# Attention plus spectral mixing on one core: folded maxima scans and eight spectral blocks moved into the attention loop

## The chip, the cores and the metric

The kernel runs on one core of one Trainium2 chip. The metric is the device time of one execution in microseconds (us); a kernel's time is the median of its runs. The core has five instruction queues that run side by side and wait for each other through semaphores: PE (TensorE, matmuls), DVE (VectorE), ACT (ScalarE), POOL (GpSimd) and SP (SyncE, which here only issues DMAs). Each queue is in order: an instruction that waits holds back everything behind it on its queue. A DMA can be issued from any of SP, ACT and POOL and stands in that queue like any other instruction.

## The reference

```python
S, D, H = 2048, 512, 32; Dh = 16
g = sigmoid((x * gate_w).sum(-1, keepdims=True))
# A: attention with 32 heads of 16
q, k, v = split_heads(x @ wqkv)
p = softmax(q @ k.T * Dh ** -0.5)
a = (p @ v merged over heads) @ wo
# B: spectral mixing, real part of a two-dimensional Fourier transform
ar = x @ dft_hid_re.T ; bi = x @ dft_hid_im.T
b = dft_seq_re @ ar - dft_seq_im @ bi
return g * a + (1 - g) * b
```

`x` is 2048 x 512. `dft_seq_re` and `dft_seq_im` are 2048 x 2048, so B is two products of 2048 x 2048 with 2048 x 512 behind two small ones. All arrays are float32.

## The kernel before

**Arithmetic.** A float32 operand that is multiplied with accuracy is split in two fp32r parts, hi (a rounding copy) and lo (raw minus hi), and a product is made of three: hi hi, hi lo, lo hi. A product over 128 rows is issued as two matmuls over rows 0 to 63 and 64 to 127 (`halves_of`, L145), which run in the array side by side into two PSUM halves. Such a pair of 512 columns is the unit in which PE time is counted below, and is called a pair. In the first part of the program each pair belongs to a "slot": `products` issues one pair and calls `beside`, which counts the slot, runs deferred actions that have come due (`after(n, f)`: do f n slots later) and sprinkles in other work.

**The maxima.** The softmax needs a shift for each query and head, the row maximum of its scores. It is computed by a pass of its own, called a scan. Heads go in 16 pairs; a pair's pass is 64 scans (`SCANS`), each of a block of 128 queries against 512 keys (`i // 4` is the query block, `i % 4` the key chunk). A scan (`scan`, L119 and L121) is two matmuls of 48 rows, one for each head of the pair (one pair in the sense above), and one DVE tensor_reduce over the 2 x 512 scores from PSUM into `mx`. After a pair's 64 scans `shift` (L134 to L138) reduces `mx` to the maxima, splits and stores them. There are 16 x 64 = 1024 scans (`TOTAL`). The rows of queries and keys that scans read are loaded from DRAM for each head pair into two 1 MB tiles of the pool `stk` by eight DMAs (`row_loads`, L87).

**Front, first half.** Projections: queries and keys transposed (`project_t`, 32 calls of 12 slots, results added, split and stored to `q_d`, `k_d`), values, and the two hidden-dimension transforms (`project_s`, 48 calls of 12 slots). Each call's two PSUM halves are evacuated by ACT and added by POOL.

**Front, second half.** The spectral product: 16 blocks of output rows in phase 0 (`dft_seq_re`) and 16 in phase 1 (`dft_seq_im`), 48 slots each. The coefficients come in units of 4 row blocks (12 slots): a 256 KB load on SP, then a cast and a subtraction on POOL (`prepare`, L246 and L247). The transformed operand lies in 32 SBUF blocks, `ah[s]` and `al[s]`; between the phases they are rewritten block by block (`split_operand`, L213 and L214, on ACT, DVE and POOL). At a block's end ACT scales both halves by 1 - g (L496, L500), POOL adds them and, in phase 1, adds the phase 0 result read back from `y_d` (L450, L452); SP stores the sum to `y_d` (`mixed`).

**Scans beside the front.** From slot 192 on, `beside` issues a scan every `PACE` = 3.9 slots (other spacings hold in a few stretches), with two PSUM tiles of two banks each, until `FRONT` = 564 scans are done.

**Attention loop.** 512 steps: 16 head pairs x 32 (`PERIODS`), each a half of the queries against a block of 128 keys for two heads. A step computes scores transposed in four matmuls (`qk2`, L543), three exponentials on ACT (one of 1024 columns, L547, two of 512, L551) and `pv` (L558). The remaining scans run here, one to a step (`next_scan`), so steps 0 to 459 have one. From step `MIX` = 461 on there is no scan; every step takes one piece of the output mixing instead (`fill`, the generator `outputs`: `mix_heads`, `mix_some`), and `pv` is issued for two steps together on every second step. The scan and the mixing share one PSUM tile of two banks (`pair_banks`). A short tail closes the program.

Of the kernel before, what the change touches and what calls it, by code (L numbers as in the profile page):

```python
# [10 lines left out]
F32 = mybir.dt.float32  # L11
F32R = mybir.dt.float32r
# [6 lines left out]
P = 128  # L19
S = 2048  # L20
# [14 lines left out]
FRONT = 564  # L35
PACE = 3.9
NWARM = 20
MIX = TOTAL - FRONT + 1
SLOW = 3


def build(tc, x, xT, wqkv, wo, wrT, wiT, cr, ci, gate, out):
    nc = tc.nc
    with ExitStack() as ctx:
        keep = ctx.enter_context(tc.tile_pool(name="keep", bufs=1))
        stk = ctx.enter_context(tc.tile_pool(name="stk", bufs=6))
        sm = ctx.enter_context(tc.tile_pool(name="sm", bufs=2))
        dram = ctx.enter_context(tc.tile_pool(name="dram", bufs=1, space=DRAM))

        q_d = [dram.tile([P, 2, S], F32, name=f"q_d{f}") for f in range(ND)]  # L50
        k_d = [dram.tile([P, 2, S], F32, name=f"k_d{f}") for f in range(ND)]
        m_d = [dram.tile([2, 4, 2, NB, 32], F32, name=f"m_d{p}") for p in range(NP)]
# [23 lines left out]
        def row_loads(p, queue):  # L76
# [4 lines left out]
            for j in range(2):  # L81
                b, r = 64 * j, slice(DH * ((2 * p + j) % 8), DH * ((2 * p + j) % 8) + DH)
                loads += [(ks[b:b + 32, :], k_d[p // 4][r, 0:1, :].to_broadcast([DH, 2, S])),
                          (qs[b:b + 32, :], q_d[p // 4][r, :, :].rearrange("e n s -> (e n) s")),
                          (ks[b + 32:b + 48, :], k_d[p // 4][r, 1, :]),
# [23 lines left out]

        def scan(n, ps):  # L110
# [4 lines left out]
            if i == 0:  # L115
                mx[p] = sm.tile([P, 2, NB, 4], F32, tag="mx", name="mx")
# [4 lines left out]
            nc.vector.tensor_reduce(mx[p][:, :, qb, c], ps, axis=AX.X, op=ALU.max)  # L121

        def shift(p):
# [6 lines left out]
            def store():  # L130
                for n, s in enumerate((hi, lo)):
                    nc.sync.dma_start(m_d[p][n].rearrange("g j b k -> (g j b) k"), s.bitcast(F32))

            return [lambda: nc.vector.tensor_reduce(m, mx[p].rearrange("p j b c -> p (j b) c"), axis=AX.X, op=ALU.max,  # L134
                                                    negate=True),
# [10 lines left out]


        seen, slots, due = [0], [0], []
        pace = [None, 0.0]
        with ExitStack() as pf:  # L150
            psf = pf.enter_context(tc.tile_pool(name="psf", bufs=2, space=PSUM))
            big = pf.enter_context(tc.tile_pool(name="big", bufs=1, reuse_waits="tile"))
            cw = pf.enter_context(tc.tile_pool(name="cw", bufs=4, reuse_waits="tile"))

            def s1():
                return psf.tile([P, 2, 512], F32, tag="s1", name="s1")
# [5 lines left out]
            def after(n, f, *args):  # L162

                due.append((slots[0] + n, len(due), f, args))
# [10 lines left out]
            def load_scan_beside(p):  # L175
                scanned[p], loads = row_loads(p, nc.scalar if p else nc.sync)
# [6 lines left out]
            def beside():  # L183
# [5 lines left out]
                pace[1] += 1.0 / pace[0]  # L189
                while seen[0] < FRONT and pace[1] >= 1.0:  # L190
                    pace[1] -= 1.0
                    n = seen[0]
                    if n % SCANS == 36:
                        load_scan_beside(n // SCANS + 1)
                    scan(n, s1())
                    seen[0] += 1
                    if seen[0] % SCANS == 0:
                        for d, part in enumerate(shift(n // SCANS)):
                            after(3 + 4 * d, part)
# [654 lines left out]
```

## Time and profile before

| | us |
|---|---|
| median of 3 runs | 1753.88 (1752.49 to 1754.19) |
| the profiled execution, its own time | 1756.16 |
| its span (first to last instruction) | 1754.4 |
| PE busy / DVE busy / ACT busy / POOL busy | 1731.9 / 1347.4 / 1166.8 / 777.5 |

Busy time of PE is not PE at its peak: matmuls are pipelined and their ends are modelled, so a stage is read by how many matmuls it got through. The three stages that matter are the first half of the front (up to 284.8 us), the second half (to 736.1 us) and the attention loop with its tail. L numbers are line numbers of the kernel before.

### The profile page before, as it was taken

Reading aid. Unit: us, or ns where it says so; the run is one execution under the profiler, and the core shown is the slowest. Engines: PE = TensorE matmul, PEld = TensorE weight load, DVE = VectorE, ACT = ScalarE, POOL = GpSimd, SP = SyncE. Lnnn points to the kernel's source line nnn. Section 1 sums busy time; section 2 is a strip of 40 time slices with the busy share of each in tenths; the row PEclk is TensorE's granted clock in tenths of the full one; section 3 lists DMA queues with packets and bytes.
Section 4 is the critical chain, followed back from the end, with each engine's and each line's share of the span. In section 5 each row is a group of like instructions: output and inputs, shape, how many; then the busy total and the mean of one; then the engine's idle time right before and its main releaser. Section 6 shows DMA issues by size and latency. Waiting matters only on the chain.

```text
span 1754.4 us, 33571 instructions
## 1 busy us (share of the span) xinstructions
PE 1731.9 (99%) x13640; PEld 988.3 (56%) x13640; DVE 1347.4 (77%) x1296; ACT 1166.8 (67%) x1894; POOL 777.5 (44%) x881
## 2 busy tenths in 40 slices
PE   8999999999999999999999999999999999999998
PEld 6987787878777787633333333333333333333554
DVE  6799999999999999866666666666666777765233
ACT  6445333000031000299999999999999999999885
POOL 3688557666677777413232322323232323323222
PEclk9999999999999999999999999999999999999999
DMA  7662455525474553633233351441433333453512
GB/s 263 224 199 74 128 156 177 138 92 133 129 188 134 136 150 112 145 61 62 58 63 61 57 99 25 87 72 42 79 66 61 65 67 72 85 108 91 138 41 100
DMA packets 119307, 185.79 MB, mean 106 GB/s; under 512 B 53184, under 2 KB 55728, under 8 KB 112240
## 3 DMA queue, kind: packets, MB, share of 16 engines
q1 hardware_dynamic: 77200, 148.96, 32.7%
q0 software_dynamic: 38496, 19.47, 5.3%
q10 hardware_dynamic: 3456, 15.21, 4.1%
q8 instruction: 107, 1.75, 0.5%
q14 instruction: 48, 0.39, 0.1%
HBM read 129.89 MB, written 53.22 MB: 104 GB/s over the span
## 4 chain that ended last, share of the span: by engine, by line
PE 80%; DVE 12%; DMA 3%; POOL 2%; issue 1%; ACT 1%; SPq 0%; DVEq 0%; ACTq 0%; POOLq 0%
PE pvb L558 27%; PE xy L145 21%; PE s L543 18%; PE s L119 11%; DVE mx L121 11%; PE s L145 3%; DMA lc<-ob 2%; POOL s L173 1%; POOL el L173 0%; DVE b L214 0%; DMA q_d<-eh 0%; DMA raws<-xT 0%; DMA raws<-wqkv 0%; POOL lc L566 0%; DVE y L645 0%
## 5 line engine op out<-in xcount | busy, mean ns | idle before, releaser
L121 DVE TENSOR_REDUCE mx<-s 128x2 f32<-128x1024 f32 x1024 | 1208.4, 1220 | 276.2 <-PE s L119 276.1
L551 ACT ACTIVATE e<-s 128x512 f32<-128x512 f32 x1024 | 630.4, 748 | 1.6 <-PE s L543 1.6
L547 ACT ACTIVATE eb<-s 128x1024 f32<-128x1024 f32 x512 | 600.2, 1172 | 23.0 <-PE s L543 23.0
L558 PE MATMUL pvb<-e,va 128*17 128x512 f32 x2048 | 528.5, 599 | 0.0
L558 PE MATMUL pvb<-eb,va 128*17 128x512 f32 x2048 | 528.3, 599 | 0.0
L543 PE MATMUL s<-qs,ks 50*128 50x512 f32 x2048 | 454.1, 442 | 0.0
L543 PEld LDWEIGHTS s<-qs,ks 50*128 50x128 f32 x2048 | 215.3, 184 | 418.4 <-ACT eb L547 389.5
L119 PE MATMUL s<-ks,qs 48*128 48x512 f32 x2048 | 418.7, 397 | 8.4 <-DVE mx L121 6.9
L496 ACT ACTIVATE tx<-xy,gm 128x512 f32<-128x512 f32 x32 | 22.1, 689 | 380.6 <-PE xy L145 329.7
L119 PEld LDWEIGHTS s<-ks,qs 48*128 48x128 f32 x2048 | 200.3, 184 | 45.5 <-DVE mx L121 20.0
L566 POOL DMA_DIRECT2D lc<-ob x124 | 63.1, 515 | 238.9 <-DVE ob L563 238.8
L558 PEld LDWEIGHTS pvb<-eb,va 128*17 128x17 f32 x2048 | 63.4, 95 | 174.9 <-issue 163.7
L573 POOL DMA_DIRECT2D r_d<-lc x31 | 18.1, 585 | 322.3 <-DVE lc L572 322.3
L145 PE MATMUL xy<-w,b 64*128 64x512 f32 x768 | 105.4, 392 | 0.2 <-ACT s L292 0.2
L645 DVE SCALAR_TENSOR_TENSOR y<-s,g,y 128x512 f32<-128x512 f32 x50 | 36.6, 748 | 81.5 <-PE s L145 80.9
L310 ACT ACTIVATE tx<-xy 128x512 f32<-128x512 f32 x48 | 28.7, 598 | 93.1 <-PE xy L145 91.5
L575 POOL DMA_DIRECT2D rb<-r_d x124 | 60.3, 493 | 54.0 <-DMA r_d<-lc 53.9
L145 PEld LDWEIGHTS xy<-w,b 64*128 64x128 f32 x768 | 72.9, 186 | 17.0 <-ACT s L292 0.7
L576 POOL TENSOR_TENSOR ob<-ob,rb 128x512 f32<-128x512 f32 x31 | 39.7, 1282 | 70.6 <-DMA rb<-r_d 68.8
L408 POOL TENSOR_TENSOR ab<-tx,ty 128x512 f32<-128x512 f32 x32 | 41.3, 1291 | 50.6 <-ACT ty L311 32.2
L558 PEld LDWEIGHTS pvb<-e,va 128*17 128x17 f32 x2048 | 63.3, 95 | 0.3 <-ACT e L551 0.3
L173 POOL TENSOR_TENSOR el<-s,eh 128x512 fp32r<-128x512 f32 x32 | 41.4, 1295 | 48.2 <-ACT eh L173 41.0
(928 smaller groups left out, 2085.8 us busy)
## 6 DMA issues: line engine op xcount, KB each, us to landing
craw<-ci SPq DMA_DIRECT2D x64, 256.0 KB
craw<-cr SPq DMA_DIRECT2D x60, 256.0 KB
ks<-k_d SPq DMA_DIRECT2D x48, 256.0 KB
qs<-q_d SPq DMA_DIRECT2D x48, 256.0 KB
ab_d<-ab SPq DMA_DIRECT2D x32, 256.0 KB
y_d<-y SPq DMA_DIRECT2D x32, 256.0 KB
o_d<-oh POOLq DMA_DIRECT2D x28, 256.0 KB, 9.8
o_d<-ol POOLq DMA_DIRECT2D x28, 256.0 KB, 15.3
```

The costliest lines, as they stand in the source:

```text
L119: nc.tensor.matmul(ps[:, j, :], qs[b:b + 48, qb * P:(qb + 1) * P], ks[b:b + 48, c * 512:(c + 1) * 512], start=True, stop=True)
L121: nc.vector.tensor_reduce(mx[p][:, :, qb, c], ps, axis=AX.X, op=ALU.max)
L145: nc.tensor.matmul(ps[j], lhs[r], rhs[r], start=first, stop=last)
L173: d[2](*d[3])
L408: nc.gpsimd.tensor_add(ab, tx, ty)
L543: nc.tensor.matmul(pss[j], ks[b:b + 50, kb * P:(kb + 1) * P], qs[b:b + 50, q0:q0 + 512], start=True, stop=True)
L547: nc.scalar.activation(e, ps, AF.Exp, scale=SCALE)
L551: nc.scalar.activation(e[j], pss[j], AF.Exp, scale=SCALE)
L558: nc.tensor.matmul(pvb[r:r + VC, :], va[:, kb, 2 * p + j, :], es[c][j], start=kb == 0, stop=kb == NB - 1, tile_position=(0, r))
L566: nc.gpsimd.dma_start(lc[32 * n:32 * n + 32, :], ob[r + DH:r + VC, :].rearrange("p (s e) -> p s e", e=16))
L575: nc.gpsimd.dma_start(rb[r:r + DH, :], r_d[p][h][n:n + 1, :].to_broadcast([DH, 512]))
L576: nc.gpsimd.tensor_mul(ob, ob, rb)
```

## The change

**Folded scans.** For head pairs 3 to 10, as far as they are scanned in the front, the maximum over two key chunks is taken by max(s1, s2) = max over columns of (relu(s1 - s2) + s2). The keys of chunk c - 1 (c odd) are replaced by the difference of chunk c - 1 and chunk c, so the matmul of an even chunk gives s1 - s2. ACT takes its relu into SBUF, and the matmul of the odd chunk is finished by one DVE tensor_tensor_reduce of 512 columns (add, then maximum, with an accumulator output) in place of a reduction. The difference keys are made in the front (`fold_keys`) and stored to a second DRAM array `kf_d`. The two heads of a pair are offset by one scan, so each folded scan issues one even and one odd matmul, one relu and one tensor_tensor_reduce, in four single PSUM banks.

**Pace.** `FRONT` becomes 692. Plain scans still go at 3.9 slots (5.2 during the key projections, 4.5 in other narrow stretches), folded ones at 2.18.

**Moved blocks.** The last eight blocks of phase 1 leave the front and become filling of the attention loop: steps 333 (`MIX`) to 460 each take three slots of them, the output mixing starts at step 461 (`OUT`) as before. Their coefficients are split on DVE, their result is taken in by two DVE scalar_tensor_tensor per block.

**Others.** Head pair 10, which is folded for 52 scans, is loaded again with plain keys at the head of the attention loop. The output weights and rows go to the operand's SBUF blocks as those come free. One key projection moves behind the query projections, and the value weights' split moves from POOL to DVE.

```diff
+LATER = 8
+FRONT = 564 + 16 * LATER
 PACE = 3.9
+FOLDED = range(3 * SCANS, FRONT)
+FOLD_PACE = 2.18
+SLOW_PACE = 5.2
+NARROW = 4.5
 MIX = TOTAL - FRONT + 1
+OUT = MIX + NB * LATER
...
+        def scan_folded(n, j, bank, pool):
+            p, i = n // SCANS, n % SCANS
+            qb, c = i // 4, i % 4
...
+            b, ps = 64 * j, bank(f"{'dk'[c % 2]}{j}")
+            nc.tensor.matmul(ps, qs[b:b + 48, qb * P:(qb + 1) * P], ks[b:b + 48, c * 512:(c + 1) * 512],
+                             start=True, stop=True)
+            if c % 2 == 0:
+                fold[j] = pool.tile([P, 512], F32, tag=f"fold{j}", name="fold")
+                nc.scalar.activation(fold[j], ps, AF.Relu)
+            else:
+                nc.vector.tensor_tensor_reduce(out=fold[j], in0=ps, in1=fold[j], scale=1.0, scalar=-3.0e38,
+                                               op0=ALU.add, op1=ALU.max, accum_out=mx[p][:, j, qb, c // 2:c // 2 + 1])
...
-                pace[1] += 1.0 / pace[0]
+                pace[1] += (PACE / FOLD_PACE if seen[0] in FOLDED else 1.0) / pace[0]
...
+                    if n not in FOLDED:
+                        done = scan_plain(n)
+                    else:
+                        scan_folded(n, 0, *beds)
+                        done = behind(n - 1)
...
+            coef = coef[:len(coef) - NU * LATER]
...
+                def fold_keys(f, c):
+                    a, b = half.pop(c - 1), half.pop(c)
+                    hi = ep.tile([P, 512], F32R, tag="eh", name="eh", bufs=3)
+                    lo = ep.tile([P, 512], F32R, tag="ty", name="fl")
+                    nc.gpsimd.tensor_sub(a, a, b)
...
+                    after(7, nc.scalar.copy, hi, a)
+                    after(12, (nc.vector if f else nc.gpsimd).tensor_sub, lo, a, hi.bitcast(F32))
+                    after(13, store, 0, hi)
+                    after(16, store, 1, lo)
...
                     def store(i, v):
                         nc.sync.dma_start(dst[f][:, i, c * 512:(c + 1) * 512], v.bitcast(F32))
+                        if folded and c % 2:
+                            nc.sync.dma_start(kf_d[f][:, i, c * 512:(c + 1) * 512], v.bitcast(F32))
...
+                psk = py.enter_context(tc.tile_pool(name="psk", bufs=1, space=PSUM, reuse_waits="tile"))
+                beds += [lambda tag: psk.tile([P, 512], F32, tag=tag, name="s"), cp]
...
-                            nc.scalar.mul(ty, pss[t][1], gm[:, t:t + 1])
-                        after(5, mixed, ph, t, yre.get(t), tx, ty)
+                            after(5, nc.scalar.mul, ty, pss[t][1], gm[:, t:t + 1])
+                        after(10, mixed, ph, t, yre.get(t), tx, ty)
...
+            def split_unit():
+                if raws:
+                    raw = raws.pop(0)
...
+                    nc.vector.tensor_copy(hi, raw)
+                    nc.vector.tensor_sub(lo, raw, hi.bitcast(F32))
+                    parts.append((hi, lo))
+
+            def spectral(t):
+                ps = pair_banks()
+                y = ap.tile([P, D], F32, tag="take", name="y", bufs=3)
+                nc.sync.dma_start(y, y_d[t // 4][:, t % 4, :])
+                for s in range(NB):
+                    if s % CS == 0:
+                        hi, lo = parts.pop(0)
+                        load_unit()
+                    if s % CS == 1:
+                        split_unit()
+                    w = s % CS
+                    for i, (c_, a_) in enumerate(((hi, ah[s]), (hi, al[s]), (lo, ah[s]))):
+                        halves_of((ps[:, 0, :], ps[:, 1, :]), c_[:, w, :], a_, s == 0 and i == 0, s == NB - 1 and i == 2)
+                    if s < NB - 1:
+                        yield
+                for j in range(2):
+                    nc.vector.scalar_tensor_tensor(y, ps[:, j, :], gm[:, t:t + 1], y, op0=ALU.mult, op1=ALU.add)
+                nc.sync.dma_start(y_d[t // 4][:, t % 4, :], y)
+                yield
...
             def outputs():
+                for t in range(NB - LATER, NB):
+                    yield from spectral(t)
                 for c in range(NC):
...
+            if FRONT % SCANS:
+                load_scan(FRONT // SCANS)
...
-                if step >= MIX - 150 and step % 8 == 0:
+                if step >= OUT - 12:
                     next(operands, None)
-                if step == MIX - 12:
+                if step in (OUT - 12, OUT - 4):
+                    output_rows((step - OUT + 12) // 8)
```

More of the change, by code (lines that the diff above doesn't have):

```diff
@@ L74, in build, with row_loads @@
         scanned, used = {}, {}
-        def row_loads(p, queue):
+        def row_loads(p, queue, keys=k_d):
             qs = stk.tile([P, S], F32R, tag="stk", name="qs")
@@ L605, in output_operands @@
                     yield
[L606 removed]
+                    w = [block(12 + 2 * n + i) for i in range(2)]
                     nc.vector.tensor_copy(w[0], raw)
@@ L629, in output_rest @@
             def output_rest(h):
-                a = [ap.tile([P, 512], F32R, name=f"or{h}{i}") for i in range(2)]
+                a = [block(24 + 2 * h + i) for i in range(2)]
                 for i in range(2):
```

148 lines of the change are left out of this document (100 added, 48 removed).

## Prediction

> **What bounds the kernel now.** I read the page's busy times first, then the two rows of its slices that change, then the busy times of the stages.
>
> ```profile
> PE 1731.9 (99%) x13640; PEld 988.3 (56%) x13640; DVE 1347.4 (77%) x1296; ACT 1166.8 (67%) x1894; POOL 777.5 (44%) x881
> ...
> DVE  6799999999999999866666666666666777765233
> ACT  6445333000031000299999999999999999999885
> ```
>
> ```profile
> 0.00:284.80 284.80, 277.83 (x2332) 230.69 (x2334) 257.40 (x261) 134.83 (x268) 174.79 (x142) 1.00 0.56 178
> 284.80:736.10 451.30, 447.43 (x3814) 358.29 (x3812) 445.69 (x408) 52.52 (x85) 308.94 (x304) 1.00 0.50 136
> 736.10:1617.50 881.40, 877.74 (x6464) 331.84 (x6464) 599.01 (x564) 877.65 (x1388) 265.72 (x395) 1.00 0.36 69
> 616.00:660.00 44.00, 44.00 (x382) 35.62 (x380) 44.00 (x40) 3.81 (x6) 31.53 (x32) 1.00 0.56 145
> 1000.00:1200.00 200.00, 200.00 (x1482) 75.75 (x1476) 135.80 (x127) 200.00 (x318) 64.29 (x96) 1.00 0.34 66
> ```
>
> The columns are the stretch, its length, and the busy time of PE, PE's weight loads, DVE, ACT and POOL with their instruction counts, then clock and DMA. A PE at 99% everywhere says little, so I go by counts. The second half of the front is 451.3 us with PE and DVE both full and ACT at 52.5. Its best stretch gets 382 matmuls through in 44 us: a pair costs 44 / 191 = 0.2304 us. The stage holds 1536 slots and 370 scans, 1906 pairs, so 439.3 us of PE; 12.0 us are lost. The attention loop has ACT at 200 of 200 us: 318 exponentials at three to a step are 106 steps, 1.887 us each (over the whole stage 1388 / 3 = 462.7 steps, 1.905 each). There the scans cost no time: DVE and PE both have room.
>
> **The front's second half, PE.** The order of the two programs' instructions shows 1152 slots there in place of 1536, and 507 scans (7 plain, 500 folded) in place of 370: 1659 pairs, 382.2 us, 57.1 less than 439.3. That is the gain if no other engine sets the rate. In the folded stretch a scan comes every 3.18 to 3.2 pairs, 0.733 us. Each scan now needs one relu on ACT and one tensor_tensor_reduce (TTR) on DVE, and the program has that as two DVE instructions: the main one of 512 columns and an accumulator read of 128x1. Neither is in this trace. The nearest rows (from the views by line, by group, the chain of waits and the timeline):
>
> ```profile
> 291.48 69.34 DVE mx L121 x61
> L173 DVE TENSOR_TENSOR s<-xy,tx x11: 678/691/694, 16.3 to 54.2; 128x512 f32<-128x512 f32 x11
> L645 DVE SCALAR_TENSOR_TENSOR y<-s,g,y x50: 735/751/752, 1621.2 to 1748.6; 128x512 f32<-128x512 f32 x50
> 1745.93 3.37 DVE L645 SCALAR_TENSOR_TENSOR y<-s,g,y 128x512 f32<-128x512 f32 x5
> 284.70 0.20 DVE L136 STREAM_TRANSPOSE mt<-m 128x32 f32<-128x32 f32 x1
> 284.82 1.19 DVE L121 TENSOR_REDUCE mx<-s 128x2 f32<-128x1024 f32 x1
> L381 ACT ACTIVATION_READ_ACCUMULATOR xg<-xg x16: 186/203/208, 126.0 to 179.3; 128x1 f32 x16
> L214 DVE TENSOR_TENSOR b<-early,b x6: 681/1383/1782, 493.0 to 503.3; 128x512 fp32r<-128x512 f32 x6
> ```
>
> Rows with three numbers give minimum, median and maximum in ns. A plain scan's reduction takes 69.34 / 61 = 1.137 us of DVE. Five scalar_tensor_tensor in a row take 3.37 us at 0.751 each, so the next starts after (3.37 - 0.75) / 4 = 0.655: 0.096 of each is hidden. A two-source op with one source in PSUM is 0.691 or 0.751, so the main part costs 0.595 to 0.655; I take the middle, 0.625. A short op lets the next start 0.12 later (284.70 to 284.82); I take that for the accumulator read, since it has the shortest row of all. A TTR is then 0.745 us. Ends: 0.595 (the read wholly hidden) and 0.751 + 0.203 = 0.954 (nothing hidden, the read as long as ACT's). The subtraction with both sources in SBUF takes up to 1.782 beside POOL, but the PSUM-sourced rows never exceed 0.752, so I charge the TTR nothing for POOL.
>
> The Trainium skill (VectorE: DVE Perf Modes, section "The DRAIN you can't avoid") says that the next DVE op does not start until the pipe of the one before is empty, and in its section on two Vector instructions with no wait between them that an op not held starts earlier. The five scalar_tensor_tensor, 0.655 apart at 0.751 each, side with the second.
>
> What else DVE has in this stage:
>
> ```profile
> L214 DVE TENSOR_TENSOR b<-early,b 128x512 fp32r<-128x512 f32 x6 | 7.5, 1283 | 0.0
> L214 DVE TENSOR_TENSOR b<-abr,b 128x512 fp32r<-128x512 f32 x6 | 6.2, 1053 | 0.9 <-POOL chi__7062 L246 0.5 <-ACT b L213 0.4
> L214 DVE TENSOR_TENSOR b<-tail,b 128x512 fp32r<-128x512 f32 x2 | 3.1, 1574 | 0.0
> L134 DVE TENSOR_REDUCE m<-mx 128x32 f32<-128x128 f32 x16 | 4.6, 286 | 0.5
> L136 DVE STREAM_TRANSPOSE mt<-m 128x32 f32<-128x32 f32 x16 | 3.3, 203 | 0.1
> L137 DVE CAST chi<-mt 128x32 fp32r<-128x32 f32 x16 | 6.7, 419 | 0.0
> L138 DVE TENSOR_TENSOR clo<-mt,chi 128x32 fp32r<-128x32 f32 x16 | 5.0, 311 | 0.1
> ```
>
> The sum for DVE: 500 x 0.745 = 372.5; 14 single-bank reductions for the 7 plain scans at about 0.6, 8.4; operand subtractions 7.5 + 6.2 + 3.1 = 16.8; eight shifts at 19.6 / 16 = 1.22, 9.8; and 16 last slots without a scan, 3.7. Together 411.2 us, against PE's 382.2. So DVE, not PE, sets this stage, and most of the PE gain is lost on it.
>
> ACT's part:
>
> ```profile
> L310 ACT ACTIVATE tx<-xy 128x512 f32<-128x512 f32 x48 | 28.7, 598 | 93.1 <-PE xy L145 91.5 <-POOL va L384 1.7
> 709.21 0.69 ACT L496 ACTIVATE tx<-xy,gm 128x512 f32<-128x512 f32 x1 [12.72 <-PE xy L145]
> 709.80 0.68 ACT L500 ACTIVATE ty<-xy,gm 128x512 f32<-128x512 f32 x1
> ```
>
> 500 relus at 0.598 are 299 us, 47 evacuations at 0.59 are 28: ACT has room in total. But each bank is single and returns after two scans, 1.47 us; matmul 0.40, relu 0.60 and about 0.15 of signals leave 0.3 us, and an evacuation ahead of a relu takes 0.59. That is up to 0.29 x 47 = 13 us of PE waiting, nothing where PE waits for DVE already. I take 5. The stage becomes 416 us, 35 less than 451.3.
>
> **The front's first half.** It has nine scans fewer (185 for 194, 2 us of PE), and eight rounds of difference keys: a subtraction on POOL, a copy on ACT, a second subtraction on DVE or POOL and four more 256 KB stores on SP's queue in each.
>
> ```profile
> 100.00:150.00 50.00, 48.94 (x413) 40.04 (x411) 48.97 (x47) 24.66 (x53) 42.88 (x35) 1.00 0.58 168
> L173 POOL TENSOR_TENSOR el<-s,eh 128x512 fp32r<-128x512 f32 x32 | 41.4, 1295 | 48.2 <-ACT eh L173 41.0 <-DMA q_d<-el 4.6 <-DMA k_d<-el 2.6
> ```
>
> A key projection takes (12 + 12 / 5.2) x 0.2304 = 3.30 us of PE; POOL has 2 x 1.295 in it, and half a round more: 3.24. It just fits, on an engine that is 43 of 50 us busy already, and DVE is full there. I take 2 us lost; ends -2 (fewer scans, all hidden) and +8 (the eight subtractions, 10 us, in the open, less 2).
>
> **The border.** The attention loop's first scan belongs to head pair 10, whose plain keys are loaded only now.
>
> ```profile
> 731.05 9.63 SPq L173 DMA_DIRECT2D y_d<-y  x2
> 735.65 0.40 PE L145 MATMUL xy<-b,clo__9776 64*128 64x512 f32 x2
> 737.68 0.50 PE L119 MATMUL s<-ks,qs 48*128 48x512 f32 x2 [1.16 <-DVE ty L498]
> 739.06 1.27 POOL L452 TENSOR_TENSOR y<-y,yre 128x512 f32<-128x512 f32 x1
> 740.77 0.57 SPq L87 DMA_DIRECT2D ks<-k_d  x1
> 744.63 0.42 SPq L87 DMA_DIRECT2D qs<-q_d  x1
> 516.27 0.38 SPq L220 DMA_DIRECT2D abr<-ab_d  x1
> 521.03 0.62 ACT L213 CAST b<-abr 128x512 fp32r<-128x512 f32 x1 [2.98 <-DMA abr<-ab_d]
> ```
>
> SP's queue has the last spectral store in front, which waits for POOL's last addition (739.06 + 1.27), so eight loads were issued from 740.77 to 745.05, 4.7 to 9 us behind the front's last matmul. In the changed program the queue has the same order, but the first scan waits for those eight. A 256 KB load was used 4.8 us after its issue at 516.27, so the last lands near 749 in this clock, where the scan ran at 737.68. Behind that scan PE holds step 1's scores, and ACT has no exponentials. I take 9 us (11 less some start-up waits that pass beneath); ends 5 and 13.
>
> **The attention loop.** Steps 333 to 460 lose their scan (one pair) and take three pairs, with `pv` for two steps at a time. Such steps exist, with six pairs of mixing to two steps, near the end (chain of waits):
>
> ```profile
> 1709.34 1.84 PE pvb L558 x16
> 1711.84 1.38 PE s L145 x12
> 1713.71 1.84 PE pvb L558 x16
> ```
>
> Two steps take 1713.71 - 1709.34 = 4.37 us, 2.185 a step; the rest of the 4.37 is the scores of two steps. So a filled step costs 0.298 more than 1.887, or 0.280 more than 1.905: 128 steps cost 37 us (35.8 to 38.1). The coefficients' split on DVE and the two scalar_tensor_tensor per block lie beside this, for DVE has no scan left there. The output mixing is the same from step 461 on.
>
> **Sum.** -35 + 2 + 9 + 37 = +13 us against the profiled execution's 1756.16, 1769; the median lies 2.3 below that execution, so 1767 us.
>
> **The rivals.** (1) PE-bound folds: the TTR costs no more than 0.70, evacuations vanish, and the stage loses no more than the 12.0 us it loses now: 394 us, with 6 at the border and 0 in the first half: -57 + 37 + 6 = -14, 1740. For it: only 0.045 us per TTR separate the forecast from it. Against: no engine would then have slack, and DVE's other 39 us have to be absorbed.
>
> (2) Nothing hidden on DVE: main op 0.691 and read 0.203 end to end, 0.894: 500 x 0.894 + 38.7 = 486, +35 + 48 = +83, 1837. It decides from a TTR of about 0.72 on, where the whole change breaks even ((451.3 - 48 - 5 - 38.7) / 500). For it: ACT's own accumulator read takes 203 ns. Against: DVE overlaps in all its rows. The Trainium skill's section "The DRAIN you can't avoid" (VectorE: DVE Perf Modes), read strictly, is this case.
>
> (3) The moved blocks really fill: 2.185 comes from the mixing's own waits, and a spectral step takes 1.89. Then the 37 us fall away and 1730 remains. Against it: the 1709 to 1718 steps have the same pairs in the same places, and PE's chain in them has no gap.
>
> **How the numbers follow.** Forecast 58%, with its own range 1750 to 1795 (a TTR of 0.71 to 0.80); rival 1 25%, rival 2 13%, rival 3 4%. The range 1733 to 1812 leaves out rival 3, the faster end of rival 1 and most of rival 2. A measurement of this kernel tells 0.2%, 3.5 us, from no change: faster 29% (rivals 1 and 3), same 9% (the lower edge of the forecast), slower 62%.
>
> **What would show it.** A TTR and its read should start 0.74 us apart in runs, with PE's folded scans waiting for DVE more than for ACT; the first spectral block moved should show two steps in 4.37 us; the first scan of the loop should wait some 9 us for a load. The prediction is wrong if the second half of the front is under 400 us, or if the TTR pair is over 0.85.

## The result and the profile after

| | before | after |
|---|---|---|
| median, us | 1754.04 (4 runs, 1752.49 to 1756.04) | 1800.10 (4 runs, 1798.88 to 1802.71) |
| ratio, 95% interval | 1 | 1.0264 [1.0246, 1.0282] |
| profiled execution, us | 1756.16 | 1800.78 |
| its span, us | 1754.4 | 1799.0 |

The change costs 46 us; 13 were forecast. L numbers are from here on those of the changed kernel, or of the experiment that a row comes from. First the page's busy times and two rows of its 40 slices, after:

```profile
PE 1731.1 (96%) x13640; PEld 1024.8 (57%) x13640; DVE 1165.8 (65%) x1893; ACT 1453.3 (81%) x2386; POOL 708.6 (39%) x808
...
DVE  6689999999998886566666666666663211212234
ACT  6444434888887786799999999999999888885885
```

PE has the same matmuls and the same busy time as before, but 68 us of the span without work where it had 22.5. DVE has lost 182 us of work and ACT has gained 287. Now the stages: stretch, length, busy time of PE, PE's weight loads, DVE, ACT and POOL with counts, then clock and DMA.

```profile
0.00:302.90 302.90, 281.46 (x2314) 225.89 (x2316) 262.90 (x261) 139.96 (x276) 184.85 (x148) 0.98 0.60 195
302.90:711.00 408.10, 400.76 (x3318) 341.53 (x3314) 366.24 (x1061) 326.65 (x569) 228.34 (x226) 1.00 0.45 128
711.00:730.60 19.60, 2.89 (x8) 1.26 (x8) 2.46 (x3) 3.53 (x5) 3.01 (x3) 0.60 0.77 132
1637.56:1660.52 22.96, 9.81 (x73) 4.82 (x76) 4.33 (x7) 8.13 (x13) 5.22 (x5) 0.70 0.73 219
440.00:484.00 44.00, 44.00 (x372) 38.09 (x370) 39.98 (x121) 36.56 (x63) 23.81 (x25) 1.00 0.42 121
```

The third and fourth rows stand out: two short stretches in which PE works 3 of 20 and 10 of 23 us. Set against the kernel before, by the same events (the last evacuation of the first half, the front's last matmul, the loop's second scan, the joint `pv` before the second step of output mixing):

| stretch | before | after | difference | forecast |
|---|---|---|---|---|
| front, first half | 284.8 | 302.9 | +18.1 | +2 |
| front, second half | 451.3 | 408.1 | -43.2 | -35 |
| border, to the second scan of the loop | 3.4 | 19.6 | +16.2 | +9 |
| loop to that `pv`, without the wait below | 878.0 | 915.7 | +37.7 | +37 |
| wait at the start of the output mixing | 0 | 14.2 | +14.2 | 0 |
| rest | 136.9 | 138.5 | +1.6 | 0 |
| span | 1754.4 | 1799.0 | +44.6 | +13 |

**The folded scans.** From the view of one tile, then the timeline of DVE (start, length, what):

```profile
L155 DVE CUSTOM_DVE_ANT_0 fold<-s,fold x500: 649/692/694, 315.8 to 707.5; 128x512 f32<-128x512 f32 x167
L155 DVE DVE_READ_ACCUMULATOR2_ANT mx<- x500: 76/83/90, 316.4 to 708.1; 128x1 f32 x167
```

```profile
444.41 0.69 DVE L155 CUSTOM_DVE_ANT_0 fold<-s,fold 128x512 f32<-128x512 f32 x1
445.03 0.09 DVE L155 DVE_READ_ACCUMULATOR2_ANT mx<- 128x1 f32 x1
445.08 0.69 DVE L155 CUSTOM_DVE_ANT_0 fold<-s,fold 128x512 f32<-128x512 f32 x1
```

The main instruction takes 0.692 us and the read 0.083, yet the next TTR starts 0.67 after the one before: each overlaps its neighbour. In the best stretch (440 to 484 above) PE is full with 372 matmuls, 0.2366 us a pair, and DVE has 4 of 44 us free.

**The wait at the output mixing.** The chain of waits around 1650, then DVE's row with what ended its idle time, then PE's timeline:

```profile
1645.25 10.29 DMA wor<-wo
...
1655.66 0.43 DVE b L713
1656.09 0.67 DVE y L781
```

```profile
1655.66 0.43 DVE L713 CAST b<-wor 128x512 fp32r<-128x512 f32 x1 [14.13 <-DMA wor<-wo]
```

```profile
1641.87 0.61 PE L652 MATMUL pvb<-eb,va 128*17 128x512 f32 x2
...
1657.59 2.07 PE L180 MATMUL s<-b,b 64*128 64x512 f32 x8 [13.15 <-DVE y L781]
...
1660.45 1.04 PE L652 MATMUL pvb<-eb,va 128*17 128x512 f32 x2
```

DVE stands for 14.13 us, from 1641.53 on, at a conversion of output weights. Their load is issued on SP only from 1643.05 to 1645.56, behind the loads of output rows and of `y`, and its last part lands 10.29 us after its issue. Behind the conversion in DVE's queue are the two scalar_tensor_tensor (y, L781) that take the last moved block out of PSUM; that PSUM tile is the one that PE's first output mixing (s, L180) needs, and behind these matmuls stands everything else on PE. Two joint `pv`, at 1641.87 and 1660.45, are 18.6 us apart instead of 4.37: 14.2 lost. (The expectations below speak of 18.6 lost. The chain of waits leaves PE at 1639.4 and doesn't show the joint `pv` at 1641.87, so the gap in it is longer than PE's.)

**The border.** The chain of waits from the front's last additions to the second scan:

```profile
714.00 1.28 POOL y L546
...
715.29 0.32 SPq L215
...
719.09 0.42 SPq L95
...
719.56 8.84 DMA qs<-q_d
...
730.61 0.80 PE s L130 x2
```

The order is the one of the forecast: last addition on POOL, store on SP, eight loads on SP, scan. The last load lands 8.84 us after its issue where 4.8 were taken.

**The first half.** One row of a tile's view (minimum, median, maximum in ns):

```profile
L172 DVE CAST chi<-mt x16: 170/177/5176, 156.9 to 1364.5; 128x32 fp32r<-128x32 f32 x16
```

One conversion of a 128x32 tile took 5.18 us where the median is 0.18. DVE's timeline with it, POOL's beside it, and the granted clock behind it:

```profile
154.57 1.22 DVE L132 TENSOR_REDUCE mx<-s 128x2 f32<-128x1024 f32 x1
155.71 0.20 DVE L171 STREAM_TRANSPOSE mt<-m 128x32 f32<-128x32 f32 x1
...
156.93 5.18 DVE L172 CAST chi<-mt 128x32 fp32r<-128x32 f32 x1
162.02 1.21 DVE L132 TENSOR_REDUCE mx<-s 128x2 f32<-128x1024 f32 x1
```

```profile
157.10 1.30 POOL L472 TENSOR_TENSOR xg<-xn,gb 128x512 f32<-128x512 f32 x1
158.36 1.27 POOL L280 TENSOR_TENSOR clo__1758<-wraw,chi__1754 128x512 fp32r<-128x512 f32 x1
159.58 1.26 POOL L476 TENSOR_TENSOR va<-tx,ty 128x512 f32<-128x512 f32 x1
160.80 1.26 POOL L472 TENSOR_TENSOR xg<-xn,gb 128x512 f32<-128x512 f32 x1
```

```profile
160.00:164.00 4.00, 0.71 (x4) 0.62 (x6) 4.00 (x4) 0.00 (x0) 2.07 (x2) 0.75 0.14 45
164.00:168.00 4.00, 4.00 (x22) 3.16 (x20) 2.86 (x4) 0.40 (x1) 0.00 (x0) 0.50 0.28 70
172.00:176.00 4.00, 4.00 (x38) 3.46 (x36) 4.00 (x4) 2.20 (x6) 2.56 (x2) 1.00 0.28 70
```

The conversion ends at 162.11, 0.05 us behind the last of a run of POOL operations that follow each other without a break (162.06), past four boundaries between them. Beside the same run the reduction at 154.57 took its usual 1.22 and the transposition at 155.71, also between SBUF tiles, 0.20. The scans' reductions wait behind it, PE behind them, and when PE starts again its clock is granted at 0.50: 22 matmuls in 4 us where 38 are usual.

A first half is read from one execution, and it varies. Six kernels share this one unchanged: the changed kernel and the runs below called weights late, plain keys early, folds alone, both waits mended and `pv` each step. It ends at 302.9, 301.2, 301.9, 301.1, 304.2 and 299.3, so a difference of less than some 5 us between two ends says little.

### The profile page after: what moved, and what is told of

Its sections match the earlier page's. It is cut to its first block, busy times and chain, and to the rows that moved or that the text cites. A ratio compares the mean times of both kernels' runs of the same rounds, so it can differ in the third digit from the quotient of the medians.

```text
span 1799.0 us, 35571 instructions
## 1 busy us (share of the span) xinstructions
PE 1731.1 (96%) x13640; PEld 1024.8 (57%) x13640; DVE 1165.8 (65%) x1893; ACT 1453.3 (81%) x2386; POOL 708.6 (39%) x808
## 4 chain that ended last, share of the span: by engine, by line
PE 61%; DMA 3%; issue 2%; DVE 2%; POOL 1%; ACT 0%; SPq 0%; DVEq 0%; POOLq 0%; ACTq 0%
PE pvb L652 26%; PE s L637 17%; PE s L180 7%; PE s L130 4%; PE xy L180 4%; PE s L149 2%; DMA lc<-ob 1%; DMA wor<-wo 1%; DMA qs<-q_d 0%; DVE mx L132 0%; DVE fold L155 0%; DMA b<-o_d 0%; DVE y L742 0%; SPq L95 0%; POOL lc L660 0%
## 5 line engine op out<-in xcount | busy, mean ns | idle before, releaser
L132 DVE TENSOR_REDUCE mx<-s 128x2 f32<-128x1024 f32 x517 | 620.3, 1223 | 225.0 <-PE s L130 224.7
L641 ACT ACTIVATE eb<-s 128x1024 f32<-128x1024 f32 x512 | 578.7, 1130 | 85.5 <-PE s L637 85.5
L645 ACT ACTIVATE e<-s 128x512 f32<-128x512 f32 x1024 | 609.4, 707 | 1.5 <-PE s L637 1.5
L652 PE MATMUL pvb<-e,va 128*17 128x512 f32 x2048 | 518.6, 600 | 0.0
L637 PE MATMUL s<-qs,ks 50*128 50x512 f32 x2048 | 428.4, 438 | 1.6 <-DVE ty L592 1.6
L155 DVE CUSTOM_DVE_ANT_0 fold<-s,fold 128x512 f32<-128x512 f32 x500 | 336.8, 690 | 34.9 <-PE s L149 17.3
L153 ACT ACTIVATE fold<-s 128x512 f32<-128x512 f32 x500 | 294.4, 602 | 77.3 <-PE s L149 53.4
L130 PE MATMUL s<-ks,qs 48*128 48x512 f32 x1034 | 217.4, 400 | 30.0 <-DMA qs<-q_d 14.2
L149 PE MATMUL s<-ks,qs 48*128 48x512 f32 x1000 | 237.6, 406 | 6.6 <-DVE mx L155 6.4
L149 PEld LDWEIGHTS s<-ks,qs 48*128 48x128 f32 x1000 | 128.9, 184 | 48.1 <-DVE mx L155 22.1
L667 POOL DMA_DIRECT2D r_d<-lc x31 | 18.1, 585 | 297.5 <-DVE lc L666 297.5
L130 PEld LDWEIGHTS s<-ks,qs 48*128 48x128 f32 x1034 | 104.1, 185 | 45.8 <-DVE mx L132 20.1
L180 PE MATMUL xy<-w,b 64*128 64x512 f32 x768 | 108.0, 398 | 0.6 <-ACT ty L401 0.6
L180 PE MATMUL s<-b,chi 64*128 64x512 f32 x542 | 85.3, 390 | 0.3 <-ACT chi L952 0.3
L180 PEld LDWEIGHTS xy<-w,b 64*128 64x128 f32 x768 | 75.4, 190 | 16.8 <-ACT ty L401 1.5
## 6 DMA issues: line engine op xcount, KB each, us to landing
o_d<-ol POOLq DMA_DIRECT2D x28, 256.0 KB, 14.2
```

The costliest lines, as they stand in the source:

```text
L130: nc.tensor.matmul(ps[:, j, :], qs[b:b + 48, qb * P:(qb + 1) * P], ks[b:b + 48, c * 512:(c + 1) * 512], start=True, stop=True)
L149: nc.tensor.matmul(ps, qs[b:b + 48, qb * P:(qb + 1) * P], ks[b:b + 48, c * 512:(c + 1) * 512], start=True, stop=True)
L153: nc.scalar.activation(fold[j], ps, AF.Relu)
L155: nc.vector.tensor_tensor_reduce(out=fold[j], in0=ps, in1=fold[j], scale=1.0, scalar=-3.0e38, op0=ALU.add, op1=ALU.max, accum_out=mx[p][:, ...
L180: nc.tensor.matmul(ps[j], lhs[r], rhs[r], start=first, stop=last)
L637: nc.tensor.matmul(pss[j], ks[b:b + 50, kb * P:(kb + 1) * P], qs[b:b + 50, q0:q0 + 512], start=True, stop=True)
```

## The experiments

Times are medians, of 2 executions in seven of the runs and of 4 to 12 in the others; the ratio is to the kernel before in the same session, with its 95% interval. The kernel before itself had medians of 1754.0 to 1756.4 in these sessions, so differences between runs of two sessions are good to some 2 us only.

| run | us | ratio |
|---|---|---|
| weights late | 1783.26 | 1.0153 [1.0124, 1.0183] |
| plain keys early | 1783.22 | 1.0153 [1.0124, 1.0182] |
| no difference keys | 1784.70 | 1.0161 [1.0124, 1.0199] |
| folds alone | 1804.43 | 1.0274 [1.0244, 1.0304] |
| both waits mended | 1769.40 | 1.0079 [1.0058, 1.0100] |
| three edits | 1767.48 | 1.0062 [1.0041, 1.0083] |
| no keys, split on POOL | 1788.09 | 1.0186 [1.0165, 1.0206] |
| `pv` each step | 1803.51 | 1.0273 [1.0247, 1.0300] |
| no keys, conversion on ACT | 1784.00 | 1.0160 [1.0145, 1.0175] |
| both waits, conversion on ACT | 1762.17 | 1.0045 [1.0031, 1.0059] |
| no keys, both small operations off DVE | 1774.46 | 1.0107 [1.0091, 1.0123] |
| all mended | 1754.47 | 0.9996 [0.9985, 1.0007] |
| all mended, four buffers | 1754.95 | 0.9999 [0.9990, 1.0008] |
| all mended, first keys on DVE | 1755.37 | 1.0001 [0.9992, 1.0009] |
| all mended, both | 1754.40 | 0.9999 [0.9990, 1.0008] |

**The output weights in two parts**, the steps around the start of the mixing left free.

```diff
-                if step >= OUT - 12:
+                if OUT - 12 <= step < OUT - 5 or step >= OUT + 6:
```

> The changed kernel, but the last three output weights (of the last two head pairs) are loaded and split from step 467 on and no longer in steps 456 to 462, behind the loads of output rows and y. Theory (DVE's queue): the 18.6 us that the loop loses around step 460 come from one DVE cast that waits 14.1 us for these weights and holds the last moved block's evacuation behind it, for which PE waits; they go, and the time is 1781 to 1785 us. Rival (the transfers themselves): the output rows and y take as long to arrive as the weights did, so the mixing waits for them in the same place: 1795 us or more.

1783.26, 17 less. One row of the stretches of this run:

```profile
1600.00:1650.00 50.00, 50.00 (x410) 25.51 (x404) 11.87 (x21) 44.32 (x70) 9.52 (x15) 1.00 0.70 193
```

PE works 50 of 50 us across the place where it stood (here at 1641). The wait was for the weights.

**Plain keys of pair 10 loaded in the front**, into the tiles that the folded pair 11 would have had.

```diff
-                scanned[p], loads = row_loads(p, nc.scalar if p else nc.sync, kf_d if p * SCANS in FOLDED else k_d)
+                if p * SCANS > FRONT:
+                    redone[p - 1], loads = row_loads(p - 1, nc.scalar)
+                else:
+                    scanned[p], loads = row_loads(p, nc.scalar if p else nc.sync, kf_d if p * SCANS in FOLDED else k_d)
...
-                load_scan(FRONT // SCANS)
+                scanned.update(redone)
```

> The changed kernel, but the plain keys of head pair 10 are loaded beside the front's last scans, in place of the needless first load of pair 11. Theory: the border's 19.6 us (against 3.4 before) are the wait for these eight loads, and the half clock behind it; they shrink to 3 to 5 us and the time to 1783 to 1787. Rival (full DMA queues): the loads of pair 11, still issued at the border, arrive too late instead, and the wait moves to step 12: 1794 or more.

1783.22, 17 less. The timeline of PE in this run:

```profile
709.91 0.39 PE L180 MATMUL xy<-b,clo__10795 64*128 64x512 f32 x1
...
714.57 0.79 PE L130 MATMUL s<-ks,qs 48*128 48x512 f32 x2
```

From the front's last matmul to the second scan it is 4.3 us instead of 19.6.

**No difference keys.** Nothing is folded, split or stored into `kf_d`; the folded scans read the plain keys, so their maxima aren't those of the reference.

```diff
-                scanned[p], loads = row_loads(p, nc.scalar if p else nc.sync, kf_d if p * SCANS in FOLDED else k_d)
+                scanned[p], loads = row_loads(p, nc.scalar if p else nc.sync)
...
-                        if folded and c % 2:
-                            nc.sync.dma_start(kf_d[f][:, i, c * 512:(c + 1) * 512], v.bitcast(F32))
...
-                        if c % 2:
-                            after(6, fold_keys, f, c)
```

> The changed kernel without the difference keys: they are neither computed nor stored, and the folded scans read the plain keys (the maxima are then not those of the reference). Theory: the 18.1 us that the front's first half loses are the price of these eight rounds on POOL, DVE and SP's queue; the half ends by 288 us, the time is 1783 to 1787. Rival (the other edits there): the order of the key projections and the value weights' split on DVE cost it; the half still ends at 298 or later, and the time is 1795 or more.

1784.70. The first half's last evacuation starts at 291.7, between the theory and its rival:

```profile
L396 ACT ACTIVATE tx<-xy x48: 590/597/600, 118.1 to 291.7; 128x512 f32<-128x512 f32 x48
```

So the keys are 11.2 of the 18.1 us, and 6.9 belong to something else.

**The folds without the moved blocks** (`LATER = 0`, `FOLD_PACE = 3.9`).

> The changed kernel with no block moved: 564 scans in the front, all 16 blocks of phase 1 there too, folded scans at the old pace of 3.9 slots, nothing filled before step 461. Theory (the moved blocks pay 43 us in the front for 33 to 37 in the loop, nearly nothing): the second half holds 1915 pairs, 441 us, and some 8 of stalls; with the first half at 303 and the border at 16 more than before the time is 1785 to 1797, close to the changed kernel's less the wait at step 460. Rival (the moved blocks are what costs): 1754 to 1765.

1804.43, outside both ranges given. Its stretches, cut at the end of each half and at the loop's second scan:

```profile
0.00:301.40 301.40, 282.95 (x2316) 231.72 (x2318) 262.49 (x261) 139.81 (x276) 185.27 (x148) 0.98 0.60 196
301.40:760.40 459.00, 452.02 (x3828) 368.92 (x3824) 286.61 (x797) 266.97 (x457) 309.46 (x305) 0.99 0.48 134
760.40:779.60 19.20, 2.88 (x8) 1.26 (x8) 2.46 (x3) 3.50 (x5) 3.00 (x3) 0.59 0.74 136
```

The first half and the border lose what they lose in the full change, so neither loss comes from the moved blocks. DVE is relieved (287 of 459 us), yet the second half takes 459.0, 7.7 more than 451.3: before, PE was as full as DVE there, and a faster maximum alone buys nothing. The weights come late here too, but PE loses less to them: from the loop's second scan to the first joint `pv` behind the start of the output mixing it is some 884 us, 6 more than before. Moving the blocks, as the change stands, takes the time from 1804.43 to 1800.10, or from 48 to 46 us over the kernel before of the same session; the intervals overlap, so no gain is shown.

**Both waits mended** (the first two edits together).

> The changed kernel with both edits of the runs before: output weights late and plain keys early. Theory (two separate waits, one at the border, one at step 460): the gains of about 17 us each add up, 1765 to 1768. Rival (one of them only hides the other, since transfers shift into the same place): 1774 or more.

1769.40. The two gains nearly add (17 and 17 by themselves, 31 together), 1.4 us above the range given.

**Three edits**: besides, no difference keys for pairs 12 to 15, which nobody reads, and the value weights' split back on POOL.

```diff
-                    folded = dst is k_d
+                    folded = dst is k_d and f < ND - 1
...
-                        load_w(wv, wqkv[:, 1024:1536], 48, nc.vector)
+                        load_w(wv, wqkv[:, 1024:1536], 48, nc.gpsimd)
```

> As e5_both_waits, and the difference keys of the last group of head pairs (12 to 15), which no folded scan reads, are neither computed nor stored, with the value weights' split back on POOL. Theory (the first half loses its time to these rounds and to that split): the first half ends at 292 to 296 instead of 302 and the time is 1756 to 1761. Rival (POOL and DVE are late for the rounds of groups 0 to 2 already): the half ends at 299 or later, 1764 or more.

1767.48, 2 us less where 8 or more were expected, with the first half ending at 302.5: the rival's outcome. The next run suggests why: the second edit may cost some 3 us rather than gain any, and the unread keys may be worth 5; the intervals are too wide to part them.

**No difference keys, value weights' split on POOL.**

> As e3_no_difference_keys (first half 291.7 us), with the value weights' split back on POOL (the maxima are again not those of the reference). Theory: that split on DVE, which is full there, makes most of the 7 us that are left over 284.8; the half ends by 287 and the time is 1779 to 1781. Rival (the order of the key projections, or the slower pace there): it stays at 290 or more.

1788.09, 3 us more than without that edit, with the first half ending at 293.7: the rival's outcome. The split's move to DVE does not hold the remaining 6.9 us. The traces of both runs without keys then showed where they are: in both, TensorE has a hole of 4.6 to 6.1 us between 146 and 152, behind the small conversion of the maxima.

**`pv` in every step** of the filled ones, instead of two at a time on every second.

```diff
-                for _ in range(min(len(pend), 1) if step < MIX else 0 if step % 2 else 2):
+                for _ in range(min(len(pend), 1) if step < OUT else 0 if step % 2 else 2):
```

> As e5_both_waits, but in the 128 filled steps pv is issued for one step in each step, as in the scan steps, and not for two in every second. Theory (PE is the bound of a filled step: pv 0.92 to 0.98, four pairs less one already counted as scores, three of filling): a filled step stays at 2.15 to 2.25 us and the time within 5 us of e5. Rival (the waits of the pattern make the 2.185): a filled step takes 1.9 to 2.0 and the time falls by 24 us or more.

1803.51, 34 us more than the run with both waits mended, where the theory had no change and its rival a gain. A stretch of 200 us of filled steps, in the changed kernel and then in this run:

```profile
1400.00:1600.00 200.00, 200.00 (x1652) 105.91 (x1648) 39.56 (x68) 178.76 (x276) 53.99 (x81) 1.00 0.40 93
```

```profile
1360.00:1560.00 200.00, 200.00 (x1469) 86.17 (x1469) 39.70 (x62) 158.36 (x245) 48.12 (x70) 1.00 0.32 76
```

276 and 245 exponentials, three to a step: 2.174 and 2.449 us a step, with PE full in both. 128 x 0.275 = 35 us, against the 34 measured. Both stretches hold 18 matmuls a step (1652 / 92 and 1469 / 81.7), and ACT is at 179 and 158 of 200 us. So PE sets the filled step, but not by the number of its matmuls alone: their order matters, and joining two `pv` saves 0.27 us a step. Why the other order is slower is not shown.

**The conversion of the maxima on ScalarE** in the front, without the difference keys.

```diff
-                    lambda: nc.vector.tensor_copy(hi, t),
+                    lambda: (nc.scalar.copy if p < FRONT // SCANS else nc.vector.tensor_copy)(hi, t),
```

> No difference keys, and in the front the conversion of a pair's maxima (chi from mt, 128x32) made by ScalarE instead of VectorE. Theory: the 7 us that the first half keeps without the difference keys (291.7 against 284.8) are this one conversion, 5.05 us at 145.65 to 150.70 in the run without the keys, where three GpSimd operations always stand ready, and the halved clock behind the 4.58 us hole that it tears into TensorE. The first half ends at 283 to 287, the time is 1776 to 1780. Rival, the order of the key projections and the slower pace cost them: the first half ends at 290 or later and the time is 1783 to 1786.

1784.00: the rival's numbers, first half to 290.5. But the cause was not the one that the rival names. DVE and POOL in this run:

```profile
145.40 3.96 DVE L173 TENSOR_TENSOR clo<-mt,chi 128x32 fp32r<-128x32 f32 x1
```

```profile
148.06 1.25 POOL L468 TENSOR_TENSOR xg<-xn,gb 128x512 f32<-128x512 f32 x1
154.32 1.28 POOL L472 TENSOR_TENSOR va<-tx,ty 128x512 f32<-128x512 f32 x1 [5.01 <-ACT ty L397]
```

With the conversion gone, the next small operation of DVE between SBUF tiles (the subtraction, otherwise 0.18 us) takes 3.96 us and again ends with POOL's run (149.36 against 149.31). The hole had only moved to it.

**Both waits mended, no unread keys, the conversion on ScalarE.**

> The changed kernel with both late loads mended, without the unread difference keys of the last four pairs, and with the conversion of the maxima on ScalarE in the front. Theory: both waits gone give 1769.4, the conversion 7 less, the unread keys 1 to 2 less: 1759 to 1762, the first half ending at 294 to 297. Rival, other waits fill the hole that the conversion leaves, since the key stores hold the same engines: 1765 to 1769, the first half ending after 300.

1762.17, just above the theory's range; but in the profiled execution, which took 1766.85, the first half ends at 301.3, as the rival says. The subtraction is still caught there (3.98 us at 155.31).

**The subtraction on GpSimd as well**, without the difference keys.

```diff
-                    lambda: nc.vector.tensor_sub(lo, t, hi.bitcast(F32)),
+                    lambda: (nc.gpsimd if p < FRONT // SCANS else nc.vector).tensor_sub(lo, t, hi.bitcast(F32)),
```

> The run without difference keys in which ScalarE makes the conversion of the maxima, and now GpSimd the subtraction behind it (clo from mt and chi, 128x32) too, in the front. That subtraction took 3.96 us on VectorE when the conversion had gone to ScalarE, and ended with GpSimd's run of seven operations, as the conversion had. Theory: the hole in TensorE belongs to any VectorE operation from SBUF to SBUF that meets such a run, and nothing of that kind is left here. TensorE's stretch 140 to 180 is full (39 us or more of 40, clock 0.98 or more instead of 0.91), the first half ends at 283 to 286 and the time is 1774 to 1779. Rival: the transposition or another operation is caught in its place, the stretch keeps a hole of 3 us or more, and the time is 1781 to 1785.

1774.46. The first half's last evacuation and the stretch 140 to 180 in this run:

```profile
L396 ACT ACTIVATE tx<-xy x48: 590/598/600, 116.2 to 282.5; 128x512 f32<-128x512 f32 x48
```

```profile
140.00:180.00 40.00, 40.00 (x346) 32.28 (x344) 39.97 (x38) 20.10 (x48) 30.61 (x26) 1.00 0.23 68
```

The hole is gone (346 matmuls in that stretch; 282 in the changed kernel, 284 without the keys alone), and the first half ends at 282.5, 9.2 us earlier than with both operations on DVE, and 2.3 before the kernel before.

**All mended**: both waits, no unread keys, both small operations off DVE in the front.

> The kernel with both late loads mended and without the unread difference keys, and the two small operations on the maxima off VectorE in the front. Theory: the same 5 to 7 us as without the keys, 1754 to 1758, the first half ending at 294 to 297, so what is left of the changed kernel's loss is the difference keys alone. Rival: 1759 to 1763.

1754.47 in 12 runs: no difference from the kernel before can be measured. The first half ends at 289.7. The chain of waits in its profiled execution (which took 1752.37):

```profile
693.71 0.70 ACT tx L593
...
697.70 0.50 PE s L130 x2
...
1612.95 1.84 PE pvb L655 x16
```

The second half of the front, to the last matmul at 693.7, is 404.0 us against 451.3. From the loop's second scan to the joint `pv` of the table it is 915.3 against 878.0: the filled steps cost 37.2.

**What is left of the difference keys**, 7.2 us (289.7 against 282.5): a fourth buffer for the rounded parts (`eh`, `bufs=4`); the first pairs' two subtractions on VectorE; and both.

```diff
-                    nc.gpsimd.tensor_sub(a, a, b)
+                    (nc.gpsimd if f else nc.vector).tensor_sub(a, a, b)
...
-                    after(12, (nc.vector if f else nc.gpsimd).tensor_sub, lo, a, hi.bitcast(F32))
+                    after(12, nc.vector.tensor_sub, lo, a, hi.bitcast(F32))
```

> The kernel with all three waits mended (1754.5, first half ending at 289.7) with four buffers for the rounded upper parts (eh) instead of three. Theory, what the difference keys still cost, 7.2 us of the first half (289.7 against 282.5 without them), comes from their stores, which hold these buffers and with them ScalarE and GpSimd: the first half ends 2 to 5 us earlier, 1749 to 1753. Rival, it comes from the engines' own time in the subtractions and conversions: within 1.5 us of 1754.5.

> The kernel with all three waits mended, the two subtractions of the first four pairs' difference keys on VectorE instead of GpSimd. In the stretch 20 to 60 the scans haven't begun, VectorE is busy 20.06 of 40 us and GpSimd 21.92, and TensorE does 34.56 against 37.35 without the difference keys. Theory, GpSimd's four operations of 1.3 us delay the first heads' queries: TensorE regains 2 to 2.8 us there, 1751 to 1753. Rival, the stores before the first scan are what is late, and it stays within 1 us of 1754.5.

> The two edits before together. If both theories hold, 1746 to 1751, below the kernel before; if neither does, 1753 to 1756.

1754.95, 1755.37 and 1754.40, the first half ending at 293.1, 290.2 and 293.0. Neither gives anything that can be measured; which part of the keys' work holds the 7.2 us stays open. No version here is faster than the kernel before.

## Why the prediction was wrong in size, point by point

**"The output mixing is the same from step 461 on."** This sentence failed, by 14.2 us of waiting and most of the 1.6 in the rest: PE comes back from the wait at a granted clock of 0.50 (1656 to 1660), and the first joint `pv` behind it takes 3.50 us instead of 1.84. The mixing's matmuls are the same, but its weights are not where they were: before, they were loaded one part every eight steps over the last 150 steps; now they use the SBUF blocks of the transformed operand, which come free only while the last moved block runs, and they come one part a step from step 449 on. The list of changes names this edit, and the working never asked whose queue it stands in. The run with the weights in two parts gave 17 us back. This is the step that the sum put at nothing without a row; the next two are terms that were mis-sized, by 16.1 and 7.2.

**"I take 2 us lost"** (first half, 18.1). The -2 in it, nine scans fewer, fits what is left when the rest is removed (282.5 against 284.8, though one such end is no better than the spread above). The difference keys cost 11.2 by their removal, beyond the +10 that was the working's price for them all in the open. The other 9.2 had no row in the working: one small DVE operation, in the maxima of the first head pair, that met a run of POOL (for the second head pair, at 237.80, the conversion took 0.17). The working costed POOL's operations by POOL's own time alone. The rows before already had the sign of it: the conversions of the maxima had a mean of 419 ns, where the quickest takes 170. The Trainium skill (SBUF — State Buffer, section "Who interferes with whom") says that DVE conversions in a two-port mode, and DVE operations with two SBUF inputs, contend with GpSimd for a shared port pair, which whoever issues first keeps for the whole instruction. The trace agrees on who suffers: the conversion (5.18 us) and the subtraction (3.96), while a scan's reduction from PSUM (1.22) and the transposition (0.20) do not. The Trainium skill speaks of a whole instruction; here the conversion let four boundaries between POOL's instructions pass, so it waited for more than one.

**"I take 9 us"** (border, 16.2). The place and the order were right, the size was not: the last of eight loads landed 8.84 us after its issue instead of the 4.8 of a single load. That is 4.0 of the 7.2 missing. Another 2.0 had been taken off for start-up waits that pass beneath; nothing of the kind shows, for the first scan came 17.5 us behind the front's last matmul, where it had come 1.6 behind it. The end that was given, 13, was too low as well.

**"So DVE, not PE, sets this stage"** (second half, 408.1 where 416 was forecast). That is wrong in the kernel's favour. A TTR takes 0.67 us of DVE's queue, not 0.745: the main part 0.62 to the read's start (0.625 was taken), the read 0.05 before the next one starts (0.12 was taken). Then DVE's sum is 500 x 0.67 + 38.7 = 374, below PE's 382. (1906 pairs at 0.2304 make 439.1, not 439.3; nothing hangs on it.) The waits say what is next: line waited for, total, times, longest.

```profile
PEld s L149 <- DVE mx L155: 22.1, 59, 1.9
PE s L149 <- DVE mx L155: 6.4, 11, 1.5
PEld s L149 <- ACT fold L153: 5.3, 17, 0.3
```

PE still waits for DVE at times, more than for ACT, as forecast, and the stage stays 26 us above its pairs' time. That the single banks are the reason is likely, but no run tests it. Of rival 2, the serial DVE, nothing is left: the Trainium skill's section "The DRAIN you can't avoid" (VectorE: DVE Perf Modes), read strictly, would have put a TTR at 0.692 + 0.083 = 0.775, and the trace shows 0.67. Rival 1 had the TTR right (0.70 or less) and the stage 14 us too short.

**"128 steps cost 37 us"** held. The chain of waits of the changed kernel has two filled steps in 1401.53 - 1397.16 = 4.37 us:

```profile
1397.16 1.84 PE pvb L652 x16
...
1399.66 1.39 PE s L180 x12
...
1401.53 1.84 PE pvb L652 x16
```

The 37.7 of the table and the 37.2 with all mended are that term; rival 3, free filling, is off. What was wrong is the picture beside it, "DVE and PE both have room" in the steps with a scan: in them the chain runs from one matmul to the next on PE without a gap, at 1.88 us a step. A moved block thus saves its pairs in the front and pays for most of them in the loop: -47 in the second half and +37 in the loop, with all mended.

The misses add up: 16.1 (first half), 14.2 (weights), 7.2 (border), 0.7 (loop) and 1.6 (rest) to the bad, 8.2 (second half) to the good: 31.6, which is 44.6 less 13.

## What to carry to other kernels

When buffers are reused, ask for every load that moves with them which instruction waits for it, on which in-order queue, and what stands behind: here one weight load stopped DVE, and through one PSUM tile PE. A short DVE conversion or subtraction between SBUF tiles is not priced by its own time when POOL runs without a break; on another engine it cost nothing that shows here. Moving work into a stage pays only if PE has room there, which busy time can't show and the chain of waits can. The chain leaves an engine where another was later, though: how long the engine itself stood is read from its timeline.

## What the hardware showed that was not expected

- A DVE conversion or subtraction on 128x32 between SBUF tiles waited for the end of POOL's unbroken run in three runs, while a transposition of the same size beside the same run took 0.20: to 162.11 against 162.06 in the changed kernel, 150.70 against 150.65 without the difference keys, 149.36 against 149.31 with the conversion on ScalarE. In the kernel before, the same conversion got through at the next boundary of POOL's instructions (0.62 us); why there and not here is open.
- After holes of some 4 us or more in the first half, PE came back at a granted clock of 0.50 for about 4 us (164 to 168, with 22 matmuls for 38), which makes a hole of 4.69 us cost more than itself. The Trainium skill (TensorE: Matmul & The Clock Gate, section "What's actually happening") has half the clock after an idle window of about 3.4 us, until one window has been busy; the rows agree.
- A tensor_tensor_reduce of 512 columns with an accumulator read, one source in PSUM, is 0.692 + 0.083 us by its rows and 0.67 us from one to the next.
